# One of two float32 squares moves from ScalarE to GpSimd in the first block of an attention-and-MLP kernel

## The chip, the cores and the metric

The kernel runs on one core of a Trainium2 chip. The metric is the device time of one execution in microseconds (us). Engines are called by their names: TensorE (PE in the profile; PEld is its weight load), VectorE (DVE), ScalarE (ACT), GpSimd (POOL) and SyncE (SP), which issues the DMAs.

## What is computed

The reference is an attention step between 512 rows and 32 states for each of 8 batches and 8 heads, and behind it two MLPs, all in float32. The first MLP is the part of this case:

```python
def _moe_ref(x, w_in, w_out):        # x: 4608 x 512, w_in: 512 x 2048, w_out: 2048 x 512
    h = x @ w_in
    r = np.maximum(h, 0.0)
    g = r * r
    return (g @ w_out).astype(np.float32)
```

The attention gives the x of the first MLP, and the second MLP has an exponential unit in place of the squared relu. The weights come as 64-bit floats.

## The kernel before, in words

**Numbers in two halves.** TensorE multiplies in a rounded 32-bit form (F32R). To keep float32's precision, each operand is held as a rounded high half and a low half (the rest). A product is three matmuls: high by low, high by high, low by high (`mm3`, L170 to L172). A helper `split` makes the two halves of a tile: ScalarE copies into the rounded form (L177), VectorE subtracts (L178).

**Blocks.** The 8 batches are 8 blocks of 512 columns. Blocks 0 to 3 go one by one through the first MLP, blocks 4 to 7 in pairs by another routine. A block has 16 steps over the 2048 hidden rows. Step f (`s1_step`) makes 128 hidden rows: six matmuls into `h` from the block's attention weights `at` and the tiles `m`. A tile `m` holds states times w1, so that x itself needs not be formed; `emit_m` makes one for four steps. Then `relu2` works on h, and two steps later (LAG) `out_step` multiplies the result `gs` by the step's rows of v1 into four accumulators `acc`, 12 matmuls.

**relu2** has four instructions: ScalarE's relu into `r` (L585); ScalarE's float32 square `g` (L587); ScalarE's square again, rounded, into the high half of `gs` (L589); VectorE's `g` minus the high half into the low half (L590). `r` and `g` have one buffer each, `gs` three.

**Conversions.** In block 0 the weights w1 and v1 are also converted from 64-bit words to float32, a piece of w1 and a piece of v1 in turn, one a step (`convert`, L232 to L241): ScalarE's scaling of the high word (L232) and its conversion of the low word (L234), a clamp (L237: on VectorE for w1, on GpSimd for v1 but its first piece), VectorE's shift (L238) and VectorE's integer addition (L241). For v1 ScalarE or VectorE then makes the rounded half (L260, L258) and VectorE the low half (L262). SyncE loads the raw words (L218) when a buffer comes free.

**What sets the order.** The program is written step by step, and a scheduler lays out each engine's own queue, which then runs in that order. `tc.issue_after(x)` asks that an instruction be issued behind instruction x. The list `pace` holds that x for the conversions: the relu of the step. Beside this, in block 0, run `at_scores`, `at_soft1` and the other parts of block 1's attention.

Of the kernel before, what the change touches and what calls it, by code (L numbers as in the profile page):

```python
# [12 lines left out]
AF = mybir.ActivationFunctionType  # L13
ALU = mybir.AluOpType
AX = mybir.AxisListType

B, H, S, NS, D = 8, 8, 512, 32, 64
# [16 lines left out]
HI, LO = 0, 1  # L34
# [75 lines left out]
def attn_mlp_kernel(ctx: ExitStack, tc: tile.TileContext, xt, xn, st, w1, v1, w2, v2, outx, outs):  # L110
# [13 lines left out]
    nc = tc.nc  # L124
# [58 lines left out]
    if True:  # L183
# [36 lines left out]
        pace, gate, added, taken = [], [], {}, []  # L220
# [335 lines left out]
        def operand_s():  # L556
            t = xc_p.tile([P, 2, KC, NST], F32R, name="sts", tag="xc")
            for k in range(2):
                split(t[:, HI, 2 * k:2 * k + 2], t[:, LO, 2 * k:2 * k + 2], stf[:, 2 * k:2 * k + 2])
            return t  # L560
# [11 lines left out]
        def s1_x(b, op, f, ps):  # L572
            sl = slice((f % 4) * P, (f % 4 + 1) * P)
            for c in range(2):
                m = m_t[b, f // 4, c]
                mm3(ps, (m[:, HI, sl], m[:, LO, sl]), (op[:, HI, c], op[:, LO, c]), c == 0, c == 1)
# [3 lines left out]
            for k in range(KC):  # L580
                mm3(ps, (w[:, HI, k], w[:, LO, k]), (op[:, HI, k], op[:, LO, k]), k == 0, k == KC - 1)

        def relu2(ps, n):
            r = g_p.tile([P, n], F32, name="r", tag="r")
            pace[:] = [nc.scalar.activation(out=r, in_=ps, func=AF.Relu)]  # L585
            g = g_p.tile([P, n], F32, name="g", tag="g")
            nc.scalar.activation(out=g, in_=r, func=AF.Square)  # L587
            gs = gs_p.tile([P, 2, n], F32R, name="gs", tag="gs")
            nc.scalar.activation(out=gs[:, HI], in_=r, func=AF.Square)  # L589
            nc.vector.tensor_tensor(out=gs[:, LO], in0=g, in1=gs[:, HI].bitcast(F32), op=ALU.subtract)  # L590
            return gs

        waiting, acc = [], []

        def s1_step(b, f, todos):

            ps = ps_s1.tile([P, S], F32, name="h", tag="s1")
            s1_x(b, ops[b], f, ps)
            waiting.append((b, f, relu2(ps, S)))
            for todo in todos:  # L600
                todo()

# [41 lines left out]
        for b in range(SINGLE):  # L644
# [49 lines left out]
            for f in range(FC):  # L694
                s1_step(b, f, bg[f])
                if len(waiting) > LAG:
                    out_step()
# [196 lines left out]
        op = operand_s()  # L894
        gs = {}
# [3 lines left out]
        for i in range(FC + LAG):  # L899
            if i < FC:  # L900
                ps = ps_x.tile([P, NST], F32, name="h", tag="x")
# [3 lines left out]
                r = eu1_p.tile([P, NST], F32, name="r", tag="eu")  # L905
                nc.scalar.activation(out=r, in_=ps, func=AF.Relu)
                g = u21_p.tile([P, NST], F32, name="g", tag="u2")
# [8 lines left out]
            f = i - LAG  # L916
# [200 lines left out]
    for n in range(B // 2):  # L1117
        g = {}
# [52 lines left out]
```

## Time and profile before

| what | value |
|---|---|
| median of 3 runs | 1310.32 us (1308.95 to 1310.94) |
| the profiled execution | 1313.85 us |
| its span in the trace | 1312.1 us |
| TensorE busy | 1292.2 us, 98% |
| VectorE busy | 945.4 us, 72% |
| ScalarE busy | 835.5 us, 64% |
| GpSimd busy | 8.8 us, 1%, 13 instructions |

The span is the time from the first to the last instruction of one execution; the execution's own time lies 1.75 us above it. Busy time is summed over an engine's instructions. Shares over the span hide that stages differ, so the rows below are taken from stretches. In a list of groups the columns are: line, engine, operation, tile names and shapes, count; then busy us and mean ns of one; then the idle time of the engine just before them, and what ended it.

### The profile page before, as it was taken

The numbers are of one execution on the slowest core, as the hardware profiler recorded it, in microseconds if no ns is written. First come the engines' busy times: TensorE is split into PE (matmuls) and PEld (weight loads), VectorE is DVE, ScalarE is ACT, GpSimd is POOL, SyncE is SP. The second block draws the span as 40 slices with busy tenths as digits, with TensorE's granted clock in tenths as the row PEclk, the third lists the DMA queues.
The fourth block names the chain that finished last, engine by engine and source line by source line (L and its number), as shares of the span: only waits on it lengthen the run. The fifth ranks groups of instructions, "written<-read, shape, count | busy, mean of one in ns | idle before, by whom it ended". The sixth has DMA issues, their size and how long they took to land.

```text
span 1312.1 us, 19392 instructions
## 1 busy us (share of the span) xinstructions
PE 1292.2 (98%) x6964; PEld 1036.4 (79%) x6964; DVE 945.4 (72%) x1327; ACT 835.5 (64%) x1347; POOL 8.8 (1%) x13
## 2 busy tenths in 40 slices
PE   7989999999999999999999999999999999999999
PEld 5667777777677777779988888888888888888898
DVE  6996968687769865985767963789546984568644
ACT  6886778677765667665577644685446743666444
POOL 0110000000000000000000000000000000000000
PEclk9999999999999999999999999999999999999999
DMA  9889888786825653589686678767786777678733
GB/s 370 312 301 336 314 288 303 260 302 234 276 96 156 192 186 117 178 281 360 216 261 195 201 209 264 224 191 211 221 276 194 208 210 233 200 211 282 227 103 110
DMA packets 135408, 305.39 MB, mean 233 GB/s; under 512 B 14352, under 2 KB 28688, under 8 KB 132240
## 3 DMA queue, kind: packets, MB, share of 16 engines
q1 hardware_dynamic: 135312, 304.14, 70.9%
q8 instruction: 56, 0.92, 0.3%
q14 instruction: 40, 0.33, 0.1%
HBM read 227.54 MB, written 76.55 MB: 232 GB/s over the span
## 4 chain that ended last, share of the span: by engine, by line
PE 85%; DVE 5%; issue 5%; DMA 2%; ACT 2%; POOL 1%; POOLq 0%; SPq 0%; DVEq 0%; ACTq 0%
PE x L43 19%; PE X L43 13%; PE z L43 10%; PE Z L43 7%; PE y L43 4%; PE h L170 4%; PE h L172 4%; PE h L171 4%; PE acc L170 3%; PE Y L43 3%; PE acc L172 3%; PE acc L171 3%; PE as L43 2%; PE mp L362 2%; PE hs L43 1%
## 5 line engine op out<-in xcount | busy, mean ns | idle before, releaser
L178 DVE TENSOR_TENSOR gp<-g,gp 128x512 fp32r<-128x512 f32 (+1 forms) x224 | 212.4, 955 | 107.1 <-ACT gp L177 106.1
L177 ACT ACTIVATE gp<-g 128x512 fp32r<-128x512 f32 (+1 forms) x224 | 187.7, 843 | 155.6 <-PE x L43 78.2
L43 PE MATMUL x<-gp,wr 128*128 128x512 f32 x1152 | 272.7, 391 | 1.0 <-ACT eu L71 1.0
L43 PEld LDWEIGHTS x<-gp,wr 128*128 128x128 f32 x1152 | 215.1, 188 | 51.6 <-ACT eu L71 2.9
L43 PE MATMUL X<-xf,wr 128*128 128x512 f32 x768 | 186.6, 390 | 0.0
L43 PEld LDWEIGHTS X<-xf,wr 128*128 128x128 f32 x768 | 143.5, 188 | 31.5 <-ACT u L957 1.1
L43 PE MATMUL z<-gp,wr 128*128 128x512 f32 x576 | 133.5, 390 | 0.0
L43 PEld LDWEIGHTS z<-gp,wr 128*128 128x128 f32 x576 | 108.0, 188 | 23.4 <-issue 0.8
L953 DVE SCALAR_TENSOR_TENSOR g<-r,g 128x512 f32<-128x512 f32 x96 | 63.9, 689 | 62.8 <-ACT r L952 62.8
L170 PE MATMUL acc<-gs,v 128*128 128x512 f32 x256 | 103.9, 406 | 4.1 <-DVE gs L590 3.4
L170 PE MATMUL h<-at,m 128*128 128x512 f32 x256 | 101.8, 398 | 0.7 <-ACT m L177 0.7
L172 PE MATMUL h<-at,m 128*128 128x512 f32 x256 | 99.8, 392 | 1.5 <-DVE m L178 1.5
L171 PE MATMUL acc<-gs,v 128*128 128x512 f32 x256 | 100.1, 391 | 0.0
L171 PE MATMUL h<-at,m 128*128 128x512 f32 x256 | 99.9, 390 | 0.0
L172 PE MATMUL acc<-gs,v 128*128 128x512 f32 x256 | 99.4, 392 | 0.4 <-DVE v L262 0.4
L43 PE MATMUL Z<-xf,wr 128*128 128x512 f32 x384 | 97.4, 389 | 0.0
L951 ACT ACTIVATE r<-g 128x512 f32<-128x512 f32 x96 | 57.6, 625 | 58.6 <-DVE g L1001 41.6
L81 DVE TENSOR_TENSOR g<-g,g 128x1024 f32<-128x1024 f32 x72 | 87.5, 1220 | 0.8
L43 PEld LDWEIGHTS Z<-xf,wr 128*128 128x128 f32 x384 | 72.1, 188 | 15.0
L952 ACT ACTIVATE r<-r 128x512 f32<-128x512 f32 x136 | 81.6, 621 | 0.7
L170 PEld LDWEIGHTS acc<-gs,v 128*128 128x128 f32 x256 | 48.0, 188 | 31.4 <-issue 10.1
L43 PE MATMUL y<-gp,wr 128*128 128x512 f32 x288 | 68.6, 389 | 0.0
(166 smaller groups left out, 1994.7 us busy)
## 6 DMA issues: line engine op xcount, KB each, us to landing
wr<-f_v SPq DMA_DIRECT2D x288, 256.0 KB, 3.0
wr<-f_w SPq DMA_DIRECT2D x224, 256.0 KB, 3.0
f_v<-wf SPq DMA_DIRECT2D x40, 512.0 KB, 3.6
raw_w<-in_w_dram SPq DMA_DIRECT2D x32, 512.0 KB, 5.3
raw_v<-in_v_dram SPq DMA_DIRECT2D x32, 512.0 KB, 6.5
f_w<-wf SPq DMA_DIRECT2D x24, 512.0 KB, 3.7
wr<-p_v SPq DMA_DIRECT2D x48, 256.0 KB, 3.5
xt<-in_xt_dram SPq DMA_DIRECT2D x8, 1024.0 KB, 6.0
```

What stands on the lines that cost most here:

```text
L43: nc.tensor.matmul(ps, wk[a], xk[b], start=start and k == 0 and i == 0, stop=last and k == len(w) - 1 and i == 2, skip_group_check=True)
L81: return lambda jj: tt(out=out[jj], in0=a[jj], in1=b[jj], op=ALU.subtract)
L170: mm(ps, w[HI], x[LO], start=first, stop=False)
L171: mm(ps, w[HI], x[HI], start=False, stop=False)
L172: mm(ps, w[LO], x[HI], start=False, stop=last)
L177: copy = nc.scalar.activation(out=hi, in_=src, func=AF.Copy)
L178: lows[:] = [nc.vector.tensor_tensor(out=lo, in0=src, in1=hi.bitcast(F32), op=ALU.subtract)]
L362: mm(ps[e][32 * k:32 * k + 32, :], st_t[b][r, k, :], x(k, r), start=True, stop=True)
L951: act(out=r, in_=h, func=AF.Relu, scale=-1.0)
L952: act(out=r, in_=r, func=AF.Exp, scale=-1.0)
L953: nc.vector.scalar_tensor_tensor(out=out, in0=r, scalar=-1.0, in1=h, op0=ALU.add, op1=ALU.max)
```

## The change

In block 0 (b is 0) GpSimd multiplies r by itself for the float32 square; in the other blocks ScalarE squares as before. In block 0 `pace` holds the rounded square, so that conversions are issued behind that and no longer behind the relu.

```diff
-        def relu2(ps, n):
+        def relu2(ps, n, b):
             r = g_p.tile([P, n], F32, name="r", tag="r")
             pace[:] = [nc.scalar.activation(out=r, in_=ps, func=AF.Relu)]
             g = g_p.tile([P, n], F32, name="g", tag="g")
-            nc.scalar.activation(out=g, in_=r, func=AF.Square)
+            if b:
+                nc.scalar.activation(out=g, in_=r, func=AF.Square)
+            else:
+                nc.gpsimd.tensor_tensor(out=g, in0=r, in1=r, op=ALU.mult)
             gs = gs_p.tile([P, 2, n], F32R, name="gs", tag="gs")
-            nc.scalar.activation(out=gs[:, HI], in_=r, func=AF.Square)
+            high = nc.scalar.activation(out=gs[:, HI], in_=r, func=AF.Square)
+            if not b:
+                pace[:] = [high]
             nc.vector.tensor_tensor(out=gs[:, LO], in0=g, in1=gs[:, HI].bitcast(F32), op=ALU.subtract)
             return gs
@@
-            waiting.append((b, f, relu2(ps, S)))
+            waiting.append((b, f, relu2(ps, S, b)))
```

Behind `relu2` the changed file's lines are five higher: the rounded square is L592 and the subtraction L595.

How the queues move is seen on three engines. First ScalarE at step 0: `r` is the relu, `gs` the high half, `w_2` and `raw_w_200` the two halves of a conversion, `v_0` the rounded half of v1's first piece.

```order
 L585 ACTIVATE r<-h 128x512
+L592 ACTIVATE gs<-r 128x512
 L232 ACTIVATE w_2_343<-raw_w_200 128x1024
-L587 ACTIVATE g<-r 128x512
-L589 ACTIVATE gs<-r 128x512
+L234 ACTIVATE raw_w_200<-raw_w_200 128x1024
 L260 ACTIVATE v_0_322<-cv 128x2x512
-L234 ACTIVATE raw_w_200<-raw_w_200 128x1024
```

The square g is gone, gs has moved ahead of the conversion, and the conversion's two halves now stand together.

Then VectorE around step 1: `v_0` is the low half of v1's first piece, `w_2` the addition of a w1 conversion, `cv` the v1 piece whose clamp GpSimd does, `gs` the subtraction, `stf` and `srs` belong to block 0's attention.

```order
 L262 TENSOR_TENSOR v_0_322<-cv,v_0_322 128x2x512
+L595 TENSOR_TENSOR gs<-g,gs 128x512
 L241 ISA w_2_343<-raw_w_200,w_2_343 128x2048
-L533 TENSOR_TENSOR srs_406<-sr_371,z_210 128x128
-L238 TENSOR_SCALAR cv<-cv 128x1024
-L590 TENSOR_TENSOR gs<-g,gs 128x512
+L542 COPY stf<-srt_435 64x4x32
+L238 TENSOR_SCALAR cv<-cv 128x1024
+L542 COPY stf<-srt_435 64x4x32
 L241 ISA cv<-raw_v_154,cv 128x2048
```

The subtraction has moved ahead of the shift L238, which waits for GpSimd's clamp, and ahead of an addition.

Last GpSimd's queue in the changed kernel from step 0 to step 4, with numbers of buffers and with the semaphores that each waits on: `g` is the square, `cv` the clamp.

```order
L590 TENSOR_TENSOR g_338<-r_336 128x512 [waits Activation_49]
L590 TENSOR_TENSOR g_357<-r_355 128x512 [waits DVE_49,Activation_49]
L237 TENSOR_SCALAR cv_366<-cv_366 128x1024 [waits Activation_49]
L590 TENSOR_TENSOR g_417<-r_415 128x512 [waits DVE_49,Activation_49]
L590 TENSOR_TENSOR g_469<-r_467 128x512 [waits DVE_49,Activation_49]
L237 TENSOR_SCALAR cv_478<-cv_478 128x1024 [waits Activation_49]
L590 TENSOR_TENSOR g_520<-r_518 128x512 [waits DVE_49,Activation_49]
```

Before, only the clamps stood there. Now two squares stand between two clamps; from the second on a square also waits for VectorE, which must have read the g before it.

## Rows read from the trace of the kernel before

**Rows 1.** Busy time of each engine in two stretches (us; x is the number of instructions).

```profile
23.70:97.30 73.60, 68.19 (x460) 47.50 (x461) 66.73 (x92) 65.56 (x95) 8.13 (x7) 1.00 0.87 317
97.30:180.00 82.70, 82.70 (x482) 63.63 (x481) 60.93 (x118) 55.44 (x98) 0.00 (x0) 1.00 0.88 320
```

**Rows 2.** TensorE's waits, 23.7 to 97.3: us in total, times, longest.

```profile
PE acc L170 <- DVE gs L590: 3.4, 6, 1.2
```

**Rows 3.** Timeline of TensorE: start, duration (us), engine, line, instruction.

```profile
33.84 0.39 PE L172 MATMUL h<-at,m 128*128 128x512 f32 x1
34.62 0.50 PE L170 MATMUL acc<-gs,v 128*128 128x512 f32 x1 [0.39 <-DVE gs L590]
```

**Rows 4.** Timeline of ScalarE, step 4 and the next relu.

```profile
45.89 0.60 ACT L585 ACTIVATE r<-h 128x512 f32<-128x512 f32 x1 [0.94 <-PE h L172]
46.39 1.15 ACT L232 ACTIVATE w<-raw_w 128x1024 f32<-128x1024 f32 x1
47.43 0.63 ACT L587 ACTIVATE g<-r 128x512 f32<-128x512 f32 x1
47.95 0.63 ACT L589 ACTIVATE gs<-r 128x512 fp32r<-128x512 f32 x1
...
49.52 0.59 ACT L585 ACTIVATE r<-h 128x512 f32<-128x512 f32 x1
```

**Rows 5.** Timeline of VectorE, a shift behind a clamp.

```profile
33.27 0.70 DVE L238 TENSOR_SCALAR cv<-cv 128x1024 int32<-128x1024 int32 x1 [0.88 <-POOL cv L237]
33.88 0.69 DVE L590 TENSOR_TENSOR gs<-g,gs 128x512 fp32r<-128x512 f32 x1
```

**Rows 6.** VectorE's groups by form, 23.7 to 97.3.

```profile
L590 DVE TENSOR_TENSOR gs<-g,gs 128x512 fp32r<-128x512 f32 x14 | 10.3, 739 | 0.5 <-ACT gs L589 0.3
L262 DVE TENSOR_TENSOR v<-cv,v 128x1024 fp32r<-128x1024 f32 x8 | 9.8, 1220 | 0.0
L241 DVE CUSTOM_DVE_ANT_0 cv<-raw_v,cv 128x2048 uint16<-128x2048 uint16 x8 | 9.8, 1219 | 0.1
L241 DVE CUSTOM_DVE_ANT_0 w<-raw_w,w 128x2048 uint16<-128x2048 uint16 x6 | 7.3, 1212 | 0.0
...
L238 DVE TENSOR_SCALAR cv<-cv 128x1024 int32<-128x1024 int32 x8 | 5.5, 692 | 4.6 <-POOL cv L237 4.6
L238 DVE TENSOR_SCALAR w<-w 128x1024 int32<-128x1024 int32 x6 | 4.1, 690 | 0.1
L237 DVE TENSOR_SCALAR w<-w 128x1024 f32<-128x1024 f32 x6 | 4.1, 686 | 1.5 <-ACT w L232 1.4
...
L501 DVE TENSOR_TENSOR t<-t,z 128x1024 f32<-128x1024 f32 x1 | 1.2, 1225 | 0.0
L491 DVE TENSOR_TENSOR t<-t,m 128x1024 f32<-128x1024 f32 x1 | 1.2, 1218 | 0.0
```

**Rows 7.** Raw loads of w1, 23.7 to 97.3: count, size, us to landing.

```profile
raw_w<-in_w_dram SPq DMA_DIRECT2D x12, 512.0 KB, 4.4
```

**Rows 8.** ScalarE's relus, 23.7 to 97.3.

```profile
L585 ACT ACTIVATE r<-h 128x512 f32<-128x512 f32 x15 | 9.1, 605 | 4.2 <-PE h L172 4.2
```

**Rows 9.** Timelines of GpSimd and VectorE around two clamps.

```profile
73.77 1.88 POOL L237 TENSOR_SCALAR cv<-cv 128x1024 f32<-128x1024 f32 x1 [12.99 <-ACT cv L232]
...
73.55 1.18 DVE L241 CUSTOM_DVE_ANT_0 w<-raw_w,w 128x2048 uint16<-128x2048 uint16 x1
74.76 1.42 DVE L590 TENSOR_TENSOR gs<-g,gs 128x512 fp32r<-128x512 f32 x1
...
59.73 1.04 POOL L237 TENSOR_SCALAR cv<-cv 128x1024 f32<-128x1024 f32 x1 [7.48 <-ACT cv L232]
...
59.50 1.21 DVE L490 TENSOR_REDUCE m<-t 128x32 f32<-128x1024 f32 x1
```

**Rows 10.** Timeline of TensorE: two waits for VectorE's low halves of m.

```profile
67.21 0.51 PE L172 MATMUL h<-at,m 128*128 128x512 f32 x1 [0.36 <-DVE m L178]
...
96.74 0.41 PE L540 MATMUL srt<-ident,srs 128*64 128x128 f32 x2 [0.93 <-DVE m L178]
```

## The prediction, on record before the change was run

> **What bounds the kernel now.** Read the busy time by stretches first. From 23.7 to 97.3 us, which is block 0's steps, TensorE is busy 68.19 of 73.60 us; in the next 82.7 us it has no gap [rows 1]. So block 0 holds 5.4 us of idle TensorE, and whatever moves its end moves everything behind it. The list of TensorE's waits says what the gaps are: 3.4 of them, in six pieces, are the output matmuls waiting for the low half of gs, which VectorE writes [rows 2]. A gap costs more than its idle time: two matmuls lie 0.78 us apart (33.84 and 34.62) where the cadence is 0.23, so 0.55 is lost against 0.39 shown [rows 3]. With 0.16 more for each, the six waits cost 3.4 + 6 x 0.16 = 4.4 us.
>
> Who is late? Both helpers are nearly full: VectorE 66.73 and ScalarE 65.56 of 73.6 us [rows 1]. ScalarE's row of instructions shows a step: relu at 45.89, a conversion at 46.39, the square g at 47.43, the rounded square gs at 47.95 [rows 4]. So gs starts 2.06 us after the relu. On VectorE the subtraction often stands behind a shift that waits for GpSimd's clamp: idle until 33.27, the shift, and only at 33.88 the subtraction [rows 5].
>
> **What the change removes.** In a converting step ScalarE loses the float32 square, 0.52 us by the distance from 47.43 to 47.95 [rows 4]. It pays a little back: gs, now directly behind the relu, reads r and can start only when the relu's 0.60 us are over, while the unrelated conversion started 0.50 after it [rows 4]. That is 0.42 us saved in each of some 13 converting steps and 0.52 in the others, about 6.5 us of ScalarE's time. The conversion itself starts 0.52 + 0.10 = 0.62 us later behind its relu; I cost that at nothing, since its second half no longer waits behind two squares. gs starts 0.60 instead of 2.06 us behind the relu. If gs were ever the only thing missing, all six waits would go: 4.4 us is the most that this part can give.
>
> **What it moves.** On VectorE the subtraction now stands ahead of the shift that waits for the clamp. At the five places that make up the 4.6 us of clamp waits [rows 6], 0.61 us of work (33.27 to 33.88 [rows 5]) now falls into the wait: 5 x 0.61 = 3.0 us filled, 1.6 left. On SyncE's queue the loads of raw weights wait for VectorE's additions, and a load of x (1024 KB) moves ahead of two of them. No conversion waits for a load in the stretch now; a raw load is issued a whole conversion ahead. I cost this at nothing; without that cover a load takes 4.4 us to land [rows 7]. ScalarE's relu has a new wait: r has one buffer, and the square must have read it. Two relus lie 3.63 us apart now (45.89 and 49.52 [rows 4]) and will lie 3.63 - 0.42 = 3.2 apart; the square is over after 0.60 + 1.22 (one VectorE instruction ahead of it) + 1.04 = 2.9. Covered, so nothing; if not, each miss delays ScalarE by some tenths.
>
> **What it adds: 15 squares on GpSimd in this stretch** (15 of 16 relus lie in it [rows 8]). GpSimd shows no tensor_tensor before. Nearest row: its clamp of 128x1024 takes 1.04 us undisturbed [rows 9]. The square reads 512 elements twice, also 1024 reads, so I take 1.04; half of it, 0.52, is the low end. GpSimd has time enough. The question is VectorE. One clamp of the trace met a VectorE instruction with two SBUF inputs: L241 ran from 73.55 to 74.73; the clamp started at 73.77 and took 1.88 instead of 1.04, ending at 75.65; VectorE's next subtraction started at 74.76 and took 1.42 instead of 0.69 [rows 9]. Each waited for the other in turn: about 0.8 us lost on GpSimd, then 0.73 on VectorE. Where the clamp lay beside a one-input reduction (59.50 to 60.71), neither was longer [rows 9]. So a square holds up VectorE if VectorE's next instruction has two SBUF inputs. These groups are 10.3 + 9.8 + 9.8 + 7.3 + 1.2 + 1.2 = 39.6 us [rows 6], 54% of 73.6. The loss: 15 x 1.04 x 0.54 = 8.4 us.
>
> VectorE has room: 73.6 - 66.73 = 6.9 us idle, of which 1.6 stays behind the clamps, so 5.3 us can take the loss. **VectorE ends 8.4 - 5.3 = 3.1 us later.** Does TensorE feel it in full? It touches VectorE's m tiles without cover: at 67.21 it waited 0.36 for one and at 96.74, the end of the stretch, 0.93 [rows 10]. Whatever VectorE loses before those points arrives in full, and the saved gs waits in between don't help, because TensorE then merely reaches the same wait sooner. **Sum: +3.1 us.** The profiled execution took 1313.85 us (span 1312.1) and would take 1317.0; the median of the runs shown is 1310.32, 3.5 us lower, and the sum on it gives 1313.4.
>
> Bounds: with 0.52 per square the loss is 15 x 0.52 x 0.54 = 4.2, less than the room, and then the gs waits decide: down to -4.4. Above, if no room can be used and more forms collide (below): 15 x 1.04 x 0.73 = +11.4. I take the middle as nearest to the one collision that the trace shows.
>
> The Trainium skill (GPSIMD Engine Reference, section 3.1) speaks against this change: a two-input elementwise operation of 2048 float32 per partition is measured there at 4497 ns, about twice VectorE. No run here shows it. An estimate by a quarter of that page's figure is 1.12 us, and with it the sum would be 15 x 1.12 x 0.54 - 5.3 = +3.8 us.
>
> **Rivals.**
>
> *More forms collide.* VectorE's shifts and clamps with one input take 0.69 us for 1024 elements where the two-input addition of that size takes 1.22 [rows 6], so they move two elements at a time, perhaps over GpSimd's way in. For: that halved time. Against: nothing in the trace, since none of them overlaps a GpSimd instruction. They are 5.5 + 4.1 + 4.1 = 13.7 us, 19%. Then 15 x 1.04 x 0.73 - 5.3 = +6.1: 1316.4 us. The Trainium skill (SBUF — State Buffer, section Who interferes with whom) says this of two-port modes, as of two SBUF inputs, and excludes reductions; the trace agrees on L241, the subtraction and the reduction, and shows nothing on the halved forms.
>
> *The squares fit (faster).* GpSimd gets its turns where VectorE idles or has one-input work, VectorE loses less than its 5.3 us (0.35 per square), and the earlier gs takes away the six waits: -4.4, 1305.9 us. For: gs starts 1.5 us sooner behind the relu, and the subtraction for which TensorE stood until 34.62 came straight after a clamp wait that the new order fills [rows 3, 5]. Against: VectorE is over 90% busy, so a GpSimd instruction seldom finds it idle.
>
> *Nothing measurable.* The gs waits go and waits for m tiles or for the low halves of v of the same size take their place: 1310.3 us. For: TensorE already waits for both kinds, 0.36 and 0.93 [rows 10].
>
> That the change doesn't do what it says can be left out: the order shows the squares on GpSimd and the conversions behind gs.
>
> **How the numbers follow.** Forecast 40%, more forms 22%, faster 24%, nothing 14%. A measurement of this kernel tells 0.2%, 2.6 us, from no change: below 1307.7 is faster, above 1312.9 slower. The forecast lies only just above that bound; of its 40 I count 28 as slower, 10 as same, 2 as faster. With the 22 that makes slower 0.50. Same is 10 + 12 of the third rival's 14 = 0.22, faster 24 + 2 + 2 = 0.28. The range runs from just below the faster case, 1305.5, to 1319.5, past the case with more forms; beyond lie the price with no room at all and a gain larger than all six waits, together about 2 in 10. Most of the chance with a sign is slower, and there the range is 1311.5 to 1319.5.
>
> **What would show it.** Right: GpSimd's squares with a spread of times, short ones near 1 us and long ones near 2; subtractions and additions on VectorE that take 0.7 us or more above 0.69 and 1.22; VectorE's busy time up by about 8 us in block 0, fewer TensorE waits for gs and longer ones for m or v; block 0's end some 3 us later. Shifts of 0.69 that grow past 1.4 would show the first rival. It is wrong if the squares all stand at one duration and VectorE's rows keep theirs, or if the block ends earlier with the gs waits gone; and it is wrong in another way if the relus wait for GpSimd.

## The result, and the profile after

| | before | after |
|---|---|---|
| median | 1309.88 us (4 runs, 1308.95 to 1310.94) | 1321.95 us (4 runs, 1320.4 to 1324.04) |
| profiled execution, its span | 1313.85, 1312.1 us | 1320.4, 1318.6 us |

The ratio is 1.0092 [1.0078, 1.0107]: the change makes the kernel 12.1 us slower. The forecast had the direction, but the time lies above its range.

The two traces are compared over equal work: from 23.7 us, where both stand at the same place, to ScalarE's relu of step 15. That relu starts at 100.45 before and at 110.77 after, so block 0 lost 10.3 us. (The rest of the program took 3.8 us less in the profiled execution of after than in that of before, whose time lies 4.0 us over its median.) Busy time in that stretch, before, with the columns of [rows 1]: length, TensorE, its weight loads, VectorE, ScalarE, GpSimd, granted clock of TensorE as a share of full speed, busy share of the DMA engines, GB/s.

```profile
23.70:100.45 76.75, 71.34 (x474) 50.08 (x475) 69.15 (x98) 65.57 (x96) 8.13 (x7) 1.00 0.88 317
```

And after:

```profile
23.70:110.77 87.07, 73.76 (x474) 51.32 (x475) 79.64 (x97) 59.08 (x81) 29.15 (x22) 0.98 0.77 279
```

ScalarE lost its 6.5 us of work, as forecast. VectorE's busy time rose by 10.5 us for the same work but one instruction of 0.4 us, about as much as the stretch got longer. Its idle time did not shrink: 76.75 - 69.15 = 7.6 before, 87.07 - 79.64 = 7.4 after. VectorE's groups by form, of the same stretch of after (against [rows 6]):

```profile
L595 DVE TENSOR_TENSOR gs<-g,gs 128x512 fp32r<-128x512 f32 x15 | 12.8, 851 | 4.8 <-POOL g L590 4.8
L262 DVE TENSOR_TENSOR v<-cv,v 128x1024 fp32r<-128x1024 f32 x8 | 12.2, 1531 | 0.1
L241 DVE CUSTOM_DVE_ANT_0 cv<-raw_v,cv 128x2048 uint16<-128x2048 uint16 x8 | 10.7, 1332 | 0.6
L241 DVE CUSTOM_DVE_ANT_0 w<-raw_w,w 128x2048 uint16<-128x2048 uint16 x6 | 9.0, 1496 | 0.1
L238 DVE TENSOR_SCALAR cv<-cv 128x1024 int32<-128x1024 int32 x8 | 7.0, 870 | 0.8 <-POOL cv L237 0.8
L178 DVE TENSOR_TENSOR m<-mp,m 128x512 fp32r<-128x512 f32 x10 | 6.5, 681 | 0.8 <-ACT m L177 0.8
L237 DVE TENSOR_SCALAR w<-w 128x1024 f32<-128x1024 f32 x6 | 5.0, 826 | 0.0
L238 DVE TENSOR_SCALAR w<-w 128x1024 int32<-128x1024 int32 x6 | 4.9, 819 | 0.0
...
```

The large groups with two SBUF inputs (L595, L262, L241) have grown, and so have the one-input forms L237 and L238, which undisturbed take 0.69 us for 1024 elements where two inputs take 1.22 (called halved below). L178, whose product `mp` comes from TensorE, has not, but it met GpSimd only once here, for 0.2 us. The waits for the clamp fell from 4.6 to 0.8 us, and a wait of 4.8 us for GpSimd's g took their place. Single meetings, GpSimd's side first:

```profile
40.10 1.18 POOL L590 TENSOR_TENSOR g<-r 128x512 f32<-128x512 f32 x1 [3.78 <-ACT r L585]
...
41.80 1.47 POOL L237 TENSOR_SCALAR cv<-cv 128x1024 f32<-128x1024 f32 x1 [0.52 <-ACT cv L232]
...
49.83 1.04 POOL L590 TENSOR_TENSOR g<-r 128x512 f32<-128x512 f32 x1 [6.57 <-ACT r L585]
53.05 1.24 POOL L590 TENSOR_TENSOR g<-r 128x512 f32<-128x512 f32 x1 [2.19 <-ACT r L585]
...
76.00 1.04 POOL L590 TENSOR_TENSOR g<-r 128x512 f32<-128x512 f32 x1 [12.27 <-DVE z L531]
...
89.13 1.15 POOL L590 TENSOR_TENSOR g<-r 128x512 f32<-128x512 f32 x1 [4.59 <-ACT r L585]
91.22 1.86 POOL L237 TENSOR_SCALAR cv<-cv 128x1024 f32<-128x1024 f32 x1 [0.94 <-ACT cv L232]
```

VectorE at the same places:

```profile
40.30 2.06 DVE L262 TENSOR_TENSOR v<-cv,v 128x1024 fp32r<-128x1024 f32 x1
42.28 1.52 DVE L595 TENSOR_TENSOR gs<-g,gs 128x512 fp32r<-128x512 f32 x1
...
50.90 0.69 DVE L595 TENSOR_TENSOR gs<-g,gs 128x512 fp32r<-128x512 f32 x1 [1.36 <-POOL g L590]
...
53.38 0.68 DVE L392 TENSOR_REDUCE mx<-sc 128x1 f32<-128x512 f32 x1
...
76.02 2.10 DVE L501 TENSOR_TENSOR t<-t,z 128x1024 f32<-128x1024 f32 x1
...
89.30 1.53 DVE L238 TENSOR_SCALAR w<-w 128x1024 int32<-128x1024 int32 x1
...
92.10 1.53 DVE L595 TENSOR_TENSOR gs<-g,gs 128x512 fp32r<-128x512 f32 x1
```

A square takes 1.04 us where VectorE stands idle (49.83). Where it has begun some 0.2 us ahead of VectorE's next instruction, that one takes 2.06 instead of 1.22, or 1.53 instead of 0.69: 0.84 us more in either form. A reduction beside a square (53.38) keeps its 0.68.

The clamps, which GpSimd did before as well, now meet VectorE too: the subtraction that fills the wait for a clamp (42.28, 92.10) runs beside that clamp and takes 1.52 or 1.53 instead of 0.69. Taking each of VectorE's instructions in the timeline against its undisturbed duration, nine of the 15 squares lengthen one, by 6.5 us in all, four of them in a halved form; six of the seven clamps lengthen one, by 5.0 us. In the kernel before one clamp did, by 0.73 [rows 9].

TensorE's waits in the stretch (us in total, times, longest):

```profile
PE acc L172 <- DVE v L262: 3.8, 3, 2.5
PE acc L170 <- ACT v L260: 3.7, 2, 2.0
PE mp L362 <- DVE w L241: 1.7, 2, 1.2
PE h L170 <- ACT m L177: 1.3, 2, 1.0
...
PE acc L170 <- DVE gs L595: 0.6, 2, 0.4
```

The 3.4 us for gs [rows 2] have become 0.6, as forecast, and waits for the conversions' results v and w stand in their place. VectorE's instructions for the next four steps' m tiles tell where the loss is handed on; before:

```profile
43.77 1.28 DVE L178 TENSOR_TENSOR m<-mp,m 128x512 fp32r<-128x512 f32 x2
...
66.47 1.28 DVE L178 TENSOR_TENSOR m<-mp,m 128x512 fp32r<-128x512 f32 x2
...
86.28 1.28 DVE L178 TENSOR_TENSOR m<-mp,m 128x512 fp32r<-128x512 f32 x2
```

After:

```profile
46.89 1.28 DVE L178 TENSOR_TENSOR m<-mp,m 128x512 fp32r<-128x512 f32 x2
...
73.07 1.29 DVE L178 TENSOR_TENSOR m<-mp,m 128x512 fp32r<-128x512 f32 x2 [0.79 <-ACT m L177]
...
96.11 1.28 DVE L178 TENSOR_TENSOR m<-mp,m 128x512 fp32r<-128x512 f32 x2
```

They are late by 3.1, 6.6 and 9.8 us, and the relu of step 15 by 10.3: each group of four steps adds some 3 us to what the one before it handed on.

A small part is TensorE's clock. Waiting for one v (L262) TensorE stood still for 2.46 us, and a little later its matmuls slowed:

```profile
64.86 0.50 PE L172 MATMUL acc<-gs,v 128*128 128x512 f32 x1 [2.46 <-DVE v L262]
...
66.58 0.63 PE L170 MATMUL acc<-gs,v 128*128 128x512 f32 x1
67.01 0.63 PE L171 MATMUL acc<-gs,v 128*128 128x512 f32 x1
```

The granted clock in two stretches around it (the figure behind GpSimd's):

```profile
62.00:66.00 4.00, 1.54 (x7) 0.95 (x6) 4.00 (x4) 1.46 (x2) 1.51 (x2) 1.00 0.99 367
...
67.00:68.00 1.00, 1.00 (x4) 0.79 (x3) 1.00 (x2) 0.00 (x0) 0.00 (x0) 0.50 0.64 262
```

TensorE was busy 1.54 of 4 us, then ran at half the clock (1.2 of 2.4 GHz): 0.43 us from matmul to matmul instead of 0.23. Seven such steps (66.16 to 69.14) cost 7 x 0.20 = 1.4 us.

### The profile page after: what moved, and what is told of

It is laid out like the page before. It is cut to its first block, busy times and chain, and to the rows that moved or that the text cites. A ratio compares the mean times of both kernels' runs of the same rounds, so it can differ in the third digit from the quotient of the medians.

```text
span 1318.6 us, 19406 instructions
## 1 busy us (share of the span) xinstructions
PE 1293.6 (98%) x6964; PEld 1036.5 (79%) x6964; DVE 955.7 (72%) x1327; ACT 828.6 (63%) x1331; POOL 30.9 (2%) x29
## 4 chain that ended last, share of the span: by engine, by line
PE 84%; DVE 5%; DMA 3%; ACT 1%; issue 1%; SPq 0%; DVEq 0%; ACTq 0%
PE x L43 19%; PE X L43 13%; PE z L43 9%; PE Z L43 6%; PE y L43 5%; PE h L170 4%; PE h L172 4%; PE h L171 4%; PE acc L170 4%; PE acc L172 3%; PE acc L171 3%; PE Y L43 3%; PE mp L362 2%; PE as L43 2%; PE hs L43 1%; DMA f_v<-wf 1%
## 5 line engine op out<-in xcount | busy, mean ns | idle before, releaser
L178 DVE TENSOR_TENSOR gp<-g,gp 128x512 fp32r<-128x512 f32 (+1 forms) x224 | 212.4, 955 | 106.8 <-ACT gp L177 105.8
L585 ACT ACTIVATE r<-h 128x512 f32<-128x512 f32 x64 | 38.0, 593 | 49.4 <-PE h L172 49.4
```

Of the source, the lines that this page charges most:

```text
L178: lows[:] = [nc.vector.tensor_tensor(out=lo, in0=src, in1=hi.bitcast(F32), op=ALU.subtract)]
```

## The experiments

Four causes stood against each other: the price that GpSimd's squares have on VectorE, the waits for g that come with them, the later conversions (the order), and, as what would speak for the change, the relief of ScalarE. Diffs are against the kernel named; medians of before stand in parentheses.

### The two halves of the change apart

**pace_only**, against after: both squares on ScalarE, conversions behind the rounded square.

```diff
-            if b:
-                nc.scalar.activation(out=g, in_=r, func=AF.Square)
-            else:
-                nc.gpsimd.tensor_tensor(out=g, in0=r, in1=r, op=ALU.mult)
+            nc.scalar.activation(out=g, in_=r, func=AF.Square)
```

> Only the second half of the change: in block 0 conversions are issued behind the rounded square, and both squares stay on ScalarE. Theory P (collisions of GpSimd's squares with VectorE's SBUF accesses cost the time): no square on GpSimd, so no slowdown; 1306 to 1313 us. Rival O (the later conversions make the v and m tiles late): most of the 12 us stays; 1316 to 1322 us.

Measured 1315.43 us (1310.55), ratio 1.0040 [1.0027, 1.0053], between the two. My "at nothing" for a later conversion does not hold where both squares stand ahead of it: VectorE's waits for the clamp rose from 4.6 to 7.0 us. In after, where one square stands ahead, square_only (next) tells no such loss.

**square_only**, against after: GpSimd's square, conversions behind the relu as before.

```diff
-            if not b:
-                pace[:] = [high]
```

> Only the first half: GpSimd squares, and conversions are issued behind the relu as before. Theory P: 1316 to 1324 us, VectorE's mean durations in block 0 raised as in the changed kernel. Rival O: about 1310 us.

Measured 1321.73 (1310.55), 1.0086 [1.0071, 1.0101], as the price had it. The square alone makes nearly all of after's loss; the later order adds nothing that can be told from it.

### The price by itself

**extra_square**, against before: ScalarE keeps both squares, the order stays, and GpSimd squares r once more into a tile that nobody reads.

```diff
             nc.scalar.activation(out=g, in_=r, func=AF.Square)
+            if not b:
+                nc.gpsimd.tensor_tensor(out=junk, in0=r, in1=r, op=ALU.mult)
...
+        junk = g_p.tile([P, S], F32, name="junk", tag="junk")
```

> The kernel before, with GpSimd's square of r added in block 0 into a tile that nobody reads; both of ScalarE's squares stay, and no engine waits for GpSimd's result but for r to be free. The other queues are as before. Theory P: the collisions alone, 1316 to 1323 us, with VectorE's 0.69 and 1.22 us rows raised. Rival W: nobody waits for it, 1309 to 1312 us.

Measured 1317.52 (1310.55), 1.0052 [1.0036, 1.0069]: the price, though nobody waits for this square. Its stretch to the relu of step 15:

```profile
23.70:108.23 84.53, 72.30 (x474) 50.14 (x475) 77.57 (x98) 66.56 (x96) 31.38 (x22) 1.00 0.81 289
```

VectorE's groups in that stretch:

```profile
L241 DVE CUSTOM_DVE_ANT_0 cv<-raw_v,cv 128x2048 uint16<-128x2048 uint16 x8 | 11.5, 1433 | 0.1
...
L241 DVE CUSTOM_DVE_ANT_0 w<-raw_w,w 128x2048 uint16<-128x2048 uint16 x6 | 10.5, 1753 | 0.0
...
L238 DVE TENSOR_SCALAR cv<-cv 128x1024 int32<-128x1024 int32 x8 | 5.5, 691 | 4.7 <-POOL cv L237 4.6
L238 DVE TENSOR_SCALAR w<-w 128x1024 int32<-128x1024 int32 x6 | 5.0, 828 | 0.1
```

VectorE's busy time rose by 77.57 - 69.15 = 8.4 us, and the stretch by 84.53 - 76.75 = 7.8. VectorE still waits 4.6 us for the clamp, as in [rows 6]: that idle time took nothing of the loss. By the timelines the squares account for 8.4 us of lengthening (ten of the 15 lengthen an instruction) and one clamp for 0.7, as before.

**no_wait**, against after: GpSimd squares all the same, but the subtraction reads r, so nobody waits for g.

```diff
-            nc.vector.tensor_tensor(out=gs[:, LO], in0=g, in1=gs[:, HI].bitcast(F32), op=ALU.subtract)
+            nc.vector.tensor_tensor(out=gs[:, LO], in0=g if b else r, in1=gs[:, HI].bitcast(F32), op=ALU.subtract)
```

> The changed kernel, GpSimd squares as there, but the subtraction reads r in place of g, so no engine waits for GpSimd's result; queues as in the changed kernel. Minus no_square it is the price of the collisions, and the changed kernel minus it the price of VectorE standing for the square. Theory P+W: about 7 us above no_square, 1311 to 1318 us, and 3 to 5 us below the changed kernel. Rival P alone: within 1 us of the changed kernel, 1321 to 1323 us.

Measured 1321.3 (1310.97), 1.0086 [1.0069, 1.0103], the price alone. The 4.8 us of waits for g are gone and the time is nearly after's: the intervals overlap, so at most a small part was the wait. (VectorE's busy time is 1.5 us higher here than in after, so the wait's own part can be that much larger.)

**no_square**, against after: as no_wait, and GpSimd does not square either.

```diff
-            g = g_p.tile([P, n], F32, name="g", tag="g")
             if b:
+                g = g_p.tile([P, n], F32, name="g", tag="g")
                 nc.scalar.activation(out=g, in_=r, func=AF.Square)
-            else:
-                nc.gpsimd.tensor_tensor(out=g, in0=r, in1=r, op=ALU.mult)
...
-            nc.vector.tensor_tensor(out=gs[:, LO], in0=g, in1=gs[:, HI].bitcast(F32), op=ALU.subtract)
+            nc.vector.tensor_tensor(out=gs[:, LO], in0=g if b else r, in1=gs[:, HI].bitcast(F32), op=ALU.subtract)
```

> The changed kernel with no float32 square at all in block 0 (the low half of gs is r minus gs, not r*r minus gs); queues of ScalarE, TensorE and VectorE as in the changed kernel, GpSimd has only the clamps. It shows what ScalarE's relief and the later conversions give without GpSimd. Theory V (VectorE held by collisions and waits for GpSimd costs the time): 1304 to 1311 us. Rival O (the order with later conversions and earlier subtractions is the loss by itself, as 5 us in pace_only): 1314 to 1318 us.

Measured 1312.99 (1310.97), 1.0018 [1.0009, 1.0028], between the two. It has after's ScalarE (59.35 us busy) and no square anywhere in block 0, and still isn't faster than before. Beside no_wait, from which only GpSimd's square is taken, it gives the price: 1321.3 - 1313.0 = 8.3 us. The stretch to the relu of step 15 in no_wait:

```profile
23.70:110.65 86.95, 73.50 (x474) 51.33 (x475) 81.10 (x97) 59.62 (x82) 29.58 (x22) 0.98 0.78 279
```

And in no_square:

```profile
23.70:102.70 79.00, 71.62 (x473) 50.14 (x474) 71.08 (x98) 59.35 (x81) 10.26 (x7) 1.00 0.85 308
```

VectorE does the same instructions, but for one of 0.4 us that falls outside no_wait's stretch, in 81.10 and in 71.08 us of busy time.

**no_square_relu**, against no_square: conversions behind the relu again.

```diff
-            if not b:
-                pace[:] = [high]
```

> As no_square, with conversions issued behind the relu as in the kernel before. Theory V: ScalarE's relief without its price; 1302 to 1309 us. Rival (ScalarE's relief was never worth anything, VectorE is the bound): 1309 to 1312 us.

Measured 1312.22 (1310.97), 1.0011 [1.0002, 1.0020]: no gain, as the rival had it, just above its range. Its stretch to the relu of step 15:

```profile
23.70:101.33 77.63, 71.27 (x473) 49.98 (x474) 72.92 (x98) 58.49 (x82) 10.20 (x7) 1.00 0.85 309
```

So taking ScalarE's square away gained nothing in either order. But VectorE's busy time rose in both trial kernels, by 1.9 us in no_square and 3.8 here, because the clamps met more of its instructions: by the timelines they lengthen them by 2.5 and 4.8 us, against 0.7 in before. What the relief would be worth without these meetings is not shown.

**half_square**, against after: a one-input operation that copies r stands where the square was.

```diff
-                nc.gpsimd.tensor_tensor(out=g, in0=r, in1=r, op=ALU.mult)
+                nc.gpsimd.tensor_scalar(out=g, in0=r, scalar1=1.0, scalar2=0.0, op0=ALU.mult, op1=ALU.max)
```

> The changed kernel with a one-input operation (r times 1, so g is r and not its square) of the same shape in place of the square on GpSimd; queues of the other engines are the same row by row. It reads half as much, about 0.5 us undisturbed by the row of the clamp. Theory P: the collisions shrink with GpSimd's time; the loss of 12 us falls to 3 to 7 us, 1313 to 1317 us. Rival W (VectorE's subtraction waits in its queue for another engine's result, whatever that engine's time): the loss falls by little, 1318 to 1322 us.

Measured 1320.24 (1310.55), 1.0078 [1.0063, 1.0093]. It was to be half the dose and was not, and the time lies in the rival's range: the operation is longer, not shorter, even where VectorE stands idle (49.85). GpSimd's timeline:

```profile
49.85 1.93 POOL L590 TENSOR_SCALAR g<-r 128x512 f32<-128x512 f32 x1 [5.94 <-ACT r L585]
...
61.79 2.29 POOL L590 TENSOR_SCALAR g<-r 128x512 f32<-128x512 f32 x1 [2.32 <-DVE t L396]
```

VectorE beside the second of them:

```profile
62.23 1.10 DVE L237 TENSOR_SCALAR w<-w 128x1024 f32<-128x1024 f32 x1
63.25 1.21 DVE L262 TENSOR_TENSOR v<-cv,v 128x1024 fp32r<-128x1024 f32 x1
```

L237 took 0.41 us more than its 0.69, and L262 nothing more. But VectorE waited 8.8 us in all for this g, so the run is a miss: two things changed at once, and it doesn't size the price.

### Waits and other engines

**late_relu**, against square_only: g has two buffers, and the subtraction is issued a step later, behind the next rounded square.

```diff
+    g2_p = pool("g2", 2)
...
-            g = g_p.tile([P, n], F32, name="g", tag="g")
+            g = g2_p.tile([P, n], F32, name="g", tag="g")
...
-            nc.vector.tensor_tensor(out=gs[:, LO], in0=g, in1=gs[:, HI].bitcast(F32), op=ALU.subtract)
+            low = lambda: nc.vector.tensor_tensor(out=gs[:, LO], in0=g, in1=gs[:, HI].bitcast(F32), op=ALU.subtract)
+            with tc.issue_after(high.ins):
+                for todo in late:
+                    todo()
+            late[:] = [] if b else [low]
+            if b:
+                low()
...
+        late = []
```

> GpSimd squares in block 0 as in the changed kernel, but conversions are issued behind the relu, g has two buffers, and the subtraction is written one step later, so that VectorE's queue has about the order of the kernel before and seldom stands at the subtraction waiting for GpSimd. Theory P+W (collisions cost about 7 us as in extra_square, the rest is VectorE standing at its queue's head for the square): 1313 to 1318 us, VectorE's wait for GpSimd's g under 1 us. Rival P alone (all of the 12 us is collisions): 1319 to 1323 us.

Measured 1320.3 (1310.64), 1.0075 [1.0059, 1.0092]: the price alone, but blurred. VectorE no longer waits for g, but one subtraction came so late that TensorE stood for it for 4.43 us and then ran at half the clock, as in after:

```profile
65.82 0.80 PE L171 MATMUL acc<-gs,v 128*128 128x512 f32 x1 [4.43 <-DVE gs L594]
66.41 0.63 PE L172 MATMUL acc<-gs,v 128*128 128x512 f32 x1
66.84 0.63 PE L173 MATMUL acc<-gs,v 128*128 128x512 f32 x1
```

**vector_square**, against after: VectorE does the square itself.

```diff
-                nc.gpsimd.tensor_tensor(out=g, in0=r, in1=r, op=ALU.mult)
+                nc.vector.tensor_tensor(out=g, in0=r, in1=r, op=ALU.mult)
```

> The changed kernel with the float32 square on VectorE instead of GpSimd (16 x 0.61 us more of VectorE's own time), conversions behind the rounded square. Theory V (what counts is how long VectorE is held, by its own work, by collisions or by waits, up to the hand-over to the next m tiles): VectorE is held 9.8 us longer, 1314 to 1320 us, no better than the changed kernel by more than its waits of 4.8 us. Rival C (a collision does harm beyond the time that it holds VectorE): 1308 to 1313 us.

Measured 1318.78 (1310.64), 1.0066 [1.0049, 1.0083]. Fifteen squares of 11.3 us in all on VectorE cost 8.1 us in the time, within what was expected of a bound by VectorE. Its stretch to the relu of step 15 is 84.59 us long, with VectorE busy for 80.37: of its idle time 4.2 us are left, so here some 3.4 of the 7.6 us took part of the load. With after at 1.0092 [1.0078, 1.0107] the intervals just overlap: handing the square to GpSimd was no cheaper for VectorE than doing it there.

**no_pool**, against before: VectorE does all clamps, GpSimd nothing.

```diff
-                clamp = nc.gpsimd if name == "v1" and i else nc.vector
+                clamp = nc.vector
```

> The kernel before with the seven clamps of v1 on VectorE, so GpSimd does nothing in block 0. Theory V: VectorE takes 7 x 0.61 = 4.3 us more and loses its clamp waits of 4.6 us and the one collision of 0.7 us; 1308 to 1311 us, about no change. Rival (clamps on GpSimd are hidden for VectorE): 1312 to 1316 us.

Measured 1312.91 (1310.64), 1.0015 [1.0005, 1.0025], in the rival's range. VectorE's busy time rose by 4.6 us (73.77) and the time by 2.3. So the idle time behind the clamps can be used in part, if the wait itself goes.

### Conversions earlier instead of later

**pace_prior**, against before: ScalarE keeps both squares, and conversions are issued behind the previous step's rounded square.

```diff
-            pace[:] = [nc.scalar.activation(out=r, in_=ps, func=AF.Relu)]
+            relu = nc.scalar.activation(out=r, in_=ps, func=AF.Relu)
+            pace[:] = [relu if b or not prior else prior[-1]]
...
...
-            nc.scalar.activation(out=gs[:, HI], in_=r, func=AF.Square)
+            prior[:] = [nc.scalar.activation(out=gs[:, HI], in_=r, func=AF.Square)]
...
+        prior = []
```

> The kernel before with conversions of block 0 issued behind the previous step's rounded square, thus earlier. Both squares stay on ScalarE. Theory O' (the conversions' chain to the next m tiles sets the three hand-overs, and pace_only lost its 5 us because conversions came later): earlier conversions give 1 to 4 us, 1306 to 1309 us, with shorter gaps from step 3 to 4, 7 to 8 and 11 to 12. Rival: gs comes later in turn and the output matmuls wait for it, 1310 to 1316 us.

Measured 1308.75 (1310.64), 0.9986 [0.9976, 0.9995]: 1.9 us faster than before, the fastest kernel of this study, though by less than the 0.2% that a single measurement tells. Two of its waits:

```profile
DVE cv L238 <- POOL cv L237: 2.7, 3, 1.0
...
PE acc L170 <- DVE gs L591: 1.2, 3, 0.7
```

Against 4.6 [rows 6] and 3.4 [rows 2]: an earlier conversion means an earlier clamp, so VectorE stands less.

**square_prior**, against pace_prior: the square on GpSimd in block 0.

```diff
-            nc.scalar.activation(out=g, in_=r, func=AF.Square)
+            if b:
+                nc.scalar.activation(out=g, in_=r, func=AF.Square)
+            else:
+                nc.gpsimd.tensor_tensor(out=g, in0=r, in1=r, op=ALU.mult)
```

> GpSimd squares as in the change, with conversions issued behind the previous step's rounded square, the order that gained in pace_prior. Theory V: the collisions and the waits stay whatever the order of the conversions; 1314 to 1320 us, above the kernel before. Rival O: with early conversions the square on GpSimd costs little; 1307 to 1312 us.

Measured 1321.97 (1310.97), 1.0087 [1.0072, 1.0102]: above what either had. The earlier order does not save GpSimd's square. Its stretch to the relu of step 15:

```profile
23.70:108.81 85.11, 72.42 (x474) 50.09 (x475) 81.15 (x98) 58.85 (x82) 33.60 (x22) 1.00 0.81 289
```

VectorE is busy for 81.15 us and idle for 4.0.

## Why the prediction was right in direction and wrong in size

**Right.** The undisturbed square took 1.04 us, as taken from the clamp. TensorE's waits for gs went. A relu never waited for GpSimd in the list of waits. The subtraction, moved ahead, filled the clamp waits, 4.6 to 0.8 (forecast 1.6), though it then ran beside the clamp at 1.5 instead of 0.69 us. VectorE's slip arrived in full at the m tiles, and the saved gs waits did not help there. That the loss by two-input forms, 8.4 us, is also what VectorE lost in extra_square is luck: two halved forms, of 1.7 us together, are in it.

**The step that failed** is "VectorE has room: [...] 5.3 us can take the loss". In after it took 0.2 us. VectorE's idle time in the stretch is 7.6 us before, 7.4 after and 84.53 - 77.57 = 7.0 in extra_square. In other orders a part of it was used, with 5.9 us left in no_wait, 4.2 in vector_square and 4.0 in square_prior, and yet these are 8 to 11 us slower than before. The room was a sum over the stretch, but it consists of waits for a clamp or a high half that ScalarE or GpSimd makes from something released by the same loop: relu, conversion, clamp, shift, m, matmuls, next relu. When VectorE slips, what it waits for slips too, and the wait stays. That the loop is why is argued; that the idle time stays is shown by after and extra_square. In no_pool, where an edit takes the waited-for work off the other engine, half of VectorE's additional work showed in the time. In after, moreover, the clamp waits that the new order filled came back as 4.8 us of waits for g. Without the room the sum is 8.4 us, 1318.7, still short of what was measured.

**The second term mis-sized** is what meets GpSimd, taken as 15 squares with a share of 0.54. The halved shifts and clamps collide as well, which was the first rival, and the prediction put GpSimd's own clamps, in the new order, at nothing: of the lengthening in after, 6.5 us lie beside squares and 5.0 beside clamps, less the 0.7 of before; VectorE's busy time rose by 10.5. So 15 x 1.04 x 0.73 = 11.4 us, the upper bound that the text gave and then cut off from the range, comes near it by luck. The rival's time, 1316.4, was wrong for the same room. The Trainium skill (SBUF — State Buffer, section Who interferes with whom) names two-port modes and two SBUF inputs as what contends, and reductions as free; these traces agree, with 1.22 to 2.06 for two inputs, an unchanged 1.21 [rows 9] and 0.68 for reductions, and 0.69 to 1.53 for the halved forms, if those are its two-port modes.

**Third**, the rival that was "the faster case" gave the earlier gs a worth of 4.4 us. no_square and no_square_relu have ScalarE's whole relief without any square's price and are 2.0 and 1.2 us slower than before. By that TensorE's gs waits were what showed last, not what bound; that VectorE stands behind them is argued, from its busy time. Why these two are slightly slower was not tried by itself; the clamps that met VectorE more often there fit it in no_square, with 1.9 us more of VectorE's busy time.

**Not foreseen** was the clock, some 1.4 us in after's execution.

Together: no_square's +2.0, the price of 8.3, and 1321.95 - 1321.3 = 0.7 between no_wait and after, which their intervals don't tell from nothing, make 11.0 us. The other 1.1 of the 12.1 is the distance between the medians of before of the two measurements (1309.88 and 1310.97).

## What to carry to other kernels

An engine's idle time need not be room: before taking a sum of gaps as a cushion, follow each wait back and see if what it waits for starts at the same engine and would come later with it. Work given to GpSimd was not off VectorE here: price it as VectorE time, 7.0 us for 15 squares that nobody waited for, and count halved one-input forms among those hit. Count what GpSimd does already, too: work moved into a wait for GpSimd's result runs beside the instruction that makes it. Relief of an engine is worth something only if its lateness bounds; leaving its work out in a trial kernel is a first test of that, before any new place is sought for it.

## What the runs showed of the hardware that was not expected

GpSimd's square of 1.04 us held VectorE up by at most 0.9 us, less the further it had got: in after, L501 began 0.02 us behind a square (76.00) and took 2.10 instead of 1.23, and L241 0.29 behind one (102.11) and took 1.86 instead of 1.22. In half_square a one-input operation of half the clamp's elements took 1.93 us beside an idle VectorE, where the clamp of 128x1024 takes 1.04 [rows 9]; yet the halved form that met it lost 0.41 us, and a two-input one nothing. So in half_square how long GpSimd's instruction lasts is not how long it holds VectorE. Why that operation is slow stays open; it wasn't tried with other operations.

TensorE's clock fell to half after a stop of 2.46 us in after (it was busy 1.54 of 4 us) and during one of 4.43 us in late_relu; the slow stretches lasted some 3 and 5 us, in which TensorE was busy throughout, and then the clock was granted in full again.
